# Opening of a gated linear-attention and GEGLU kernel: queries of two tiles by chunk, wq ahead of x tile 2, gate vector ahead of wk 1

## Chip, cores, metric

One Trainium2 chip, one core. The metric is the device time of one execution in microseconds; runs of a kernel are compared with runs of another from the same rounds on the same chip.

## The reference, cut to what matters

In outline (the attention is written as one call here):

```python
g = sigmoid((x * gate_w).sum(-1, keepdims=True))          # x: 2048 x 640, bf16
q, k, v = split(x @ wqkv)                                  # wqkv: 640 x 1920, 32 heads of 20
phi = lambda t: where(t > 0, t + 1, exp(t)) + 1e-6
a = linear_attention(phi(q), phi(k), v) @ wo
b = (gelu(x @ w_gate) * (x @ w_up)) @ w_down               # 640 x 1728, 1728 x 640
out = g * a + (1 - g) * b
```

Only the first 16 of 274 us matter here: the products of x with the key part (wk) and the query part (wq) of wqkv. The rows of wk and wq come in five chunks of 128 (wk 0 to 4, wq 0 to 4), because the 640-long contraction takes five matmuls. x is cut in 16 tiles of 128 rows, each wanted transposed. The gate vector becomes one more column of wq, which is why it is needed before the queries.

## The kernel before: the parts that the change touches

Each `P.op` puts an instruction into one engine's queue, in program order, and derives its semaphore waits. `eng="act"` puts a load into ScalarE's queue; the others go into SyncE's.

```python
NQ = 4                                     # tiles whose keys and queries are computed separately
...
# ScalarE: touch (a tiny first load), wk 1, wk 2, [table load], gate vector
# SyncE:   x 0, wk 0, x 1 (transposing load), wk 3, wk 4, x 2, x 3 (transposing), wq 0..4, x 4.. (transposing)
load_x(0); load_wk(0); load_xT(1); load_wk(3); load_wk(4)
load_wk(1, "act"); load_wk(2, "act")
P.op("act", lambda e: e.activation(eg[:, 0:1], zero, ACT.Exp), writes=[r_eg[0]])
P.op("dve", lambda e: e.memset(gw_sb, 0.0), writes=[r_gw])
dma_in(gw_sb[0:5, :], gate_w.rearrange("(k p) -> k p", p=128), [r_gw], eng="act")
for i in range(2, NQ): load_xT(i)
for k in range(KC):    load_wq(k)
for i in range(NQ, NT): load_xT(i)
...
warm(5, 512); warm(1, 128)                 # matmuls on constants, to bring TensorE's clock up
T(0, [0], 7); T(0, [1, 2, 3, 4], 6)        # x tile 0 is transposed by TensorE
warm(2, 128)
for k in range(3): KM(0, [k])              # keys of tile 0: a pair of matmuls (512 + 128 columns) per chunk
for k in range(3): KM(1, [k])              # keys of tile 1
KM(0, [3]); KM(1, [3]); gate_col(); KM(0, [4]); KM(1, [4])
for n in range(2 * NQ):
    if n in (2, 3): KM(n, ALLK)            # keys of tiles 2 and 3
    if n == NQ:
        for k in ALLK: QM(NQ, [k]); QM(NQ + 1, [k])   # queries of tiles 0 and 1, chunk by chunk
    if n > NQ + 1: QM(n, ALLK)             # queries of tiles 2 and 3
    phi1(n); phi2(n)                       # exp on ScalarE, the rest of phi on VectorE
for i in range(NQ, NT): KQ(i)              # fused tiles: keys and queries in 15 wide matmuls
```

## Time and profile before

| | before |
|---|---|
| time, median (range) of 6 runs | 274.00 us (273.52 to 275.16) |
| span of the profiled run | 272.6 us |
| TensorE busy | 267.6 us, 98% |
| first key pair / first fused tile starts | 4.45 us / 16.30 us |

The page of the kernel before: span, TensorE's busy time, and the engines of the chain of work that ended last.

```profile
span 272.6 us, 3416 instructions
PE 267.6 (98%) x1341; PEld 127.9 (47%) x1367; DVE 140.8 (52%) x247; ACT 75.9 (28%) x132; POOL 30.0 (11%) x28
PE 96%; DMA 1%; SPq 1%; issue 1%; DVE 0%
```

TensorE (PE) is the bound. A change can win only by removing stalls of PE. Here are its instructions in order of time, in the opening of the kernel before: start, duration, engine, line, operation, shapes, count, and in brackets the idle time before and what ended it. L453 is the wide matmul of a key pair, L539 a fused tile.

```profile
4.45 0.58 PE L453 MATMUL ps<-pool 128*128 128x512 bf16 x1 [0.48 <-DMA pool<-in_A_wqkv_dram]
...
4.93 0.51 PE L453 MATMUL ps<-pool 128*128 128x512 bf16 x1
...
5.34 0.38 PE L453 MATMUL ps<-pool 128*128 128x512 bf16 x1
...
5.61 0.38 PE L453 MATMUL ps<-pool 128*128 128x512 bf16 x1
...
7.27 0.38 PE L453 MATMUL ps<-pool 128*128 128x512 bf16 x1
...
8.12 0.39 PE L453 MATMUL ps<-pool 128*128 128x512 bf16 x1 [0.42 <-DMA pool<-in_A_x_dram]
...
16.30 1.03 PE L539 MATMUL ps<-pool 128*128 128x512 bf16 x4
```

Durations of matmuls overlap; the distance from start to start is the pace. A pair at full pace takes 0.27 us (5.34 to 5.61). Chunks 1 and 2 of wk were there when PE asked at 4.93 and 5.34 us (no wait shown). After the last key pair of tiles 0 and 1 (7.27 + 0.27 = 7.54) PE stood until 8.12 us for x tile 2: 0.58 us, the stall that the change aims at.

The queues that issue loads, SyncE's first, then ScalarE's, same kernel and columns:

```profile
1.71 1.30 SPq L353 DMA_TRANSPOSE pool<-in_A_x_dram  x1
3.06 1.04 SPq L341 DMA_DIRECT2D pool<-in_A_wqkv_dram  x2
4.14 2.53 SPq L353 DMA_TRANSPOSE pool<-in_A_x_dram  x2
6.72 2.48 SPq L341 DMA_DIRECT2D pool<-in_A_wqkv_dram  x5
```

```profile
1.24 0.93 ACTq L341 DMA_DIRECT2D pool<-in_A_wqkv_dram  x2
...
2.27 0.57 ACTq L341 DMA_DIRECT2D pool<-in_gate_w_dram  x1
```

And what the 16 DMA engines carried in the stretch from 3.6 to 4.2 us: queue, packets, MB, share of the 16 engines' time. q1 is SyncE's queue, q10 ScalarE's (wk 1 and 2, 256 packets in all).

```profile
DMA packets 215, 0.22 MB, mean 370 GB/s; under 512 B 46, under 2 KB 215, under 8 KB 215
...
q10 hardware_dynamic: 177, 0.20, 93.6%
q1 hardware_dynamic: 38, 0.02, 10.3%
```

### The profile page before, as it was taken

What the parts mean: (1) busy time and instruction counts of PE and PEld (TensorE: products, weight loads), DVE (VectorE), ACT (ScalarE), POOL (GpSimd) and SP (SyncE); (2) the same over time, 40 slices, a digit from 0 to 9 for tenths busy, and PEclk for the clock granted to TensorE, in tenths of its full rate; (3) what the DMA queues carried; (4) which work ended last, traced back from release to release, by engine and by line L of the source; (5) the groups of instructions that cost most, each with busy time, mean ns of one, the idle gap of its engine ahead of it and who ended that gap; (6) DMA issues with size and microseconds to landing.
All of it is one profiled execution on the core that took longest, in us unless ns stands there. A gap on an engine that the chain in (4) does not pass through costs nothing.

```text
span 272.6 us, 3416 instructions
## 1 busy us (share of the span) xinstructions
PE 267.6 (98%) x1341; PEld 127.9 (47%) x1367; DVE 140.8 (52%) x247; ACT 75.9 (28%) x132; POOL 30.0 (11%) x28
## 2 busy tenths in 40 slices
PE   8999999999999999999999999999999999999997
PEld 3555555544445454444444444444444444444444
DVE  1678989997233335999999999634210000000200
ACT  2455555210422453232222233224011122121021
POOL 5000000003240002242332422000000000000000
DMA  7976999600200011514121221273031110110211
GB/s 192 202 115 127 346 399 388 140 2 19 58 19 2 23 50 51 192 34 49 26 48 25 49 48 27 60 219 105 5 77 38 41 38 19 38 41 19 58 58 41
DMA packets 42864, 23.78 MB, mean 87 GB/s; under 512 B 32223, under 2 KB 41439, under 8 KB 42719
## 3 DMA queue, kind: packets, MB, share of 16 engines
q1 hardware_dynamic: 42517, 23.22, 31.9%
q10 hardware_dynamic: 330, 0.33, 0.3%
q8 instruction: 11, 0.18, 0.3%
q14 instruction: 6, 0.05, 0.1%
HBM read 13.83 MB, written 2.63 MB: 60 GB/s over the span
## 4 chain that ended last, share of the span: by engine, by line
PE 96%; DMA 1%; SPq 1%; issue 1%; DVE 0%
PE ps L700 41%; PE ps L864 23%; PE ps L539 12%; PE ps L596 6%; PE ps L843 4%; PE ps L468 2%; PE ps L811 2%; PE ps L678 2%; PE ps L599 1%; DMA pool<-in_A_x_dram 1%; PE ps L453 1%; PE ps L824 1%; SPq L341 1%; PE ps L721 1%; SPq L353 0%
## 5 line engine op out<-in xcount | busy, mean ns | idle before, releaser
L700 PE MATMUL ps<-pool 128*128 128x512 bf16 x510 | 113.0, 379 | 0.5
L700 PEld LDWEIGHTS ps<-pool 128*128 128x128 bf16 x520 | 50.5, 98 | 60.0
L864 PE MATMUL ps<-pool 128*128 128x512 bf16 (+2 forms) x300 | 62.4, 366 | 0.3
L706 ACT ACTIVATE pool<-ps 128x512 f32<-128x512 f32 x52 | 31.0, 597 | 73.1 <-PE ps L700 73.1
L708 DVE TENSOR_TENSOR pool<-ps,pool 128x512 bf16<-128x512 f32 x52 | 34.7, 689 | 31.7 <-PE ps L700 30.4
L864 PEld LDWEIGHTS ps<-pool 128*128 128x128 bf16 x306 | 29.2, 98 | 33.4 <-issue 0.4
L847 DVE TENSOR_TENSOR pool<-ps,pool 128x512 bf16<-128x512 f32 x4 | 2.8, 690 | 61.5 <-PE ps L843 61.5
L539 PE MATMUL ps<-pool 128*128 128x512 bf16 (+1 forms) x176 | 32.5, 343 | 0.2
L754 POOL TENSOR_TENSOR pool<-pool 128x640 f32<-128x640 bf16 x16 | 22.4, 1404 | 73.0 <-DVE pool L756 65.6
L871 ACT ACTIVATE pool<-ps,pool 128x512 bf16<-128x512 f32 (+1 forms) x16 | 10.9, 680 | 68.6 <-PE ps L864 68.6
L539 PEld LDWEIGHTS ps<-pool 128*128 128x128 bf16 x180 | 17.6, 98 | 15.0
L558 DVE SCALAR_TENSOR_TENSOR pool<-ps,pool 128x128 bf16<-128x128 f32 (+2 forms) x36 | 21.7, 602 | 2.1
L549 ACT ACTIVATE pool<-ps 128x640 bf16<-128x640 f32 x24 | 16.9, 703 | 15.8 <-DVE pool L558 9.3
L596 PE MATMUL ps<-pool 128*128 128x512 bf16 x76 | 19.2, 379 | 0.1
L764 DVE TENSOR_TENSOR pool<-pool 128x640 bf16<-128x640 bf16 x16 | 13.2, 826 | 0.6
L762 DVE TENSOR_SCALAR pool<-pool 128x32 f32<-128x32 f32 x16 | 12.8, 802 | 0.6
L756 DVE TENSOR_REDUCE pool<-pool 128x32 f32<-128x640 f32 x16 | 12.9, 808 | 0.0
L644 DVE TENSOR_TENSOR pool<-pool 128x640 f32<-128x640 f32 x14 | 11.6, 826 | 0.5
L843 PE MATMUL ps<-pool 128*128 128x512 bf16 x51 | 11.5, 379 | 0.1
L646 POOL PARTITION_ALL_REDUCE pool<-pool x1 | 4.0, 3971 | 61.0 <-DVE pool L644 61.0
L596 PEld LDWEIGHTS ps<-pool 128*128 128x128 bf16 x78 | 7.0, 98 | 7.3
L555 DVE TENSOR_SCALAR pool<-pool 128x640 bf16<-128x640 bf16 x24 | 7.9, 327 | 1.7 <-ACT pool L549 0.4
(70 smaller groups left out, 124.1 us busy)
## 6 DMA issues: line engine op xcount, KB each, us to landing
out_dram<-pool SPq DMA_DIRECT2D x19, 128.0 KB, 1.7
pool<-in_B_w_gate_dram SPq DMA_DIRECT2D x1, 2080.0 KB, 14.8
pool<-in_B_w_up_dram SPq DMA_DIRECT2D x1, 2080.0 KB, 18.0
pool<-in_A_wqkv_dram SPq DMA_DIRECT2D x8, 160.0 KB, 3.1
pool<-in_A_x_dram SPq DMA_DIRECT2D x1, 1280.0 KB, 9.2
pool<-in_A_x_dram SPq DMA_DIRECT2D x1, 1120.0 KB, 6.3
pool<-in_B_w_down_dram SPq DMA_DIRECT2D x1, 1120.0 KB, 6.4
pool<-omg_row SPq DMA_DIRECT2D x1, 1024.0 KB, 4.8
```

Of the source, the lines that this page charges most:

```text
L539: last = e.matmul(ps[:, b + p, 0:c1 - c0], xT[:, k, i * 128:(i + 1) * 128], wkq[:, k, c0:c1], start=(k == 0), stop=(k == KC - 1))
L549: P.op("act", lambda e: e.activation(e_buf[m], ps_flat[:, o:o + 640], ACT.Exp), reads=banks, writes=[r_e[m]])
L558: P.op("dve", lambda e, c0=c0, c1=c1: e.scalar_tensor_tensor(dst[:, c0:c1], ps_flat[:, o + c0:o + c1], 1.0 + EPS, e_buf[m][:, c0:c1], ALU. ...
L596: last = e.matmul(ps[:, b, :], pk[i][:, c * 128:(c + 1) * 128], x_aug[:, i, 0:512], start=(i == 0), stop=(i == NT - 1))
L700: last = e.matmul(ps[:, b, :], w[:, k, fc * 128:(fc + 1) * 128], xT[:, k, j * 512:(j + 1) * 512], start=(k == 0), stop=(k == KC - 1))
L706: P.op("act", lambda e: e.activation(ge[n], ps[:, gb, :], ACT.Gelu_apprx_tanh), reads=[bank[gb]], writes=[r_ge[n]])
L708: P.op("dve", lambda e: e.tensor_tensor(hT[fc][:, j * 512:(j + 1) * 512], ps[:, ub, :], ge[n], ALU.mult), reads=[bank[ub], r_ge[n]], write ...
L754: P.op("pool", lambda e: e.tensor_tensor(tmp[n], pq[i], z_b, ALU.mult), reads=[r_pq[i], r_zb], writes=[r_tmp[n]])
L756: P.op("dve", lambda e: e.tensor_reduce(den[n], tmp[n].rearrange("p (h d) -> p h d", h=32), AX.X, ALU.add), reads=[r_tmp[n]], writes=[r_de ...
L764: P.op("dve", lambda e: e.tensor_tensor(pq[i].rearrange("p (h d) -> p h d", h=32), pq[i].rearrange("p (h d) -> p h d", h=32), den[n].unsqu ...
L843: last = e.matmul(ps[:, b, :], wd[:, fc, 512:640], hT[fc][:, j * 512:(j + 1) * 512], start=False, stop=(fc == NFC - 2), skip_group_check=True)
L864: last = e.matmul(ps[:, pb, 0:c1 - c0], lhs, rhs, start=False, stop=(q == len(rows) - 1), skip_group_check=True)
```

## The change

The intent: PE has no use for x tile 2 before the queries of tiles 0 and 1, so fetch wq first, compute those queries right after the keys, and let x tiles 2 and 3 join the fused tiles. The gate vector is fetched earlier, because the queries now come earlier.

```diff
-NQ = 4
+NQ = 2
@@ loads
             P.op("act", lambda e: e.dma_start(touch[0:16, 0:4], A_wqkv[0:128:8, 640:644]),
                  writes=[P.res("touch")], dma=new_dma_key())
+            P.op("dve", lambda e: e.memset(gw_sb, 0.0), writes=[r_gw])
+            dma_in(gw_sb[0:5, :], gate_w.rearrange("(k p) -> k p", p=128), [r_gw], eng="act")
             load_x(0)
             load_wk(0)
             load_xT(1)
 ... (wk 3, wk 4; wk 1, wk 2 on ScalarE; the first activation)
-            P.op("dve", lambda e: e.memset(gw_sb, 0.0), writes=[r_gw])
-            dma_in(gw_sb[0:5, :], gate_w.rearrange("(k p) -> k p", p=128), [r_gw], eng="act")
-            for i in range(2, NQ):
-                load_xT(i)
             for k in range(KC):
                 load_wq(k)
-            for i in range(NQ, NT):
+            for i in range(2, NT):
                 load_xT(i)
@@ matmuls
             for n in range(2 * NQ):
-                if n in (2, 3):
-                    KM(n, ALLK)
                 if n == NQ:
                     for k in ALLK:
                         QM(NQ, [k])
                         QM(NQ + 1, [k])
-                if n > NQ + 1:
-                    QM(n, ALLK)
                 phi1(n)
                 phi2(n)
```

More of the change, by code (lines that the diff above doesn't have):

```diff
@@ L347, in load_x, with load_wk @@
                 dma_in(x_aug[:, i, 0:640], A_x[0, i * 128:(i + 1) * 128, :], [r_xn[i]], eng=eng)
-            def load_wk(k, eng="sp", after=()):
-                dma_in(wk[:, k, :], A_wqkv[k * 128:(k + 1) * 128, 640:1280], [r_wk[k]], reads=after, eng=eng)
+            def load_wk(k, eng="sp"):
+                dma_in(wk[:, k, :], A_wqkv[k * 128:(k + 1) * 128, 640:1280], [r_wk[k]], eng=eng)
             def load_xT(i, after=()):
@@ L355, in load_xT, with load_wq @@
                      reads=list(after), writes=[r_xT[i]], dma=new_dma_key())
-            def load_wq(k, eng="sp"):
-                dma_in(wq[:, k, 0:640], A_wqkv[k * 128:(k + 1) * 128, 0:640], [r_wq[k]], eng=eng)
+            def load_wq(k):
+                dma_in(wq[:, k, 0:640], A_wqkv[k * 128:(k + 1) * 128, 0:640], [r_wq[k]])
             P.op("act", lambda e: e.dma_start(touch[0:16, 0:4], A_wqkv[0:128:8, 640:644]),
                  writes=[P.res("touch")], dma=new_dma_key())
+            P.op("dve", lambda e: e.memset(gw_sb, 0.0), writes=[r_gw])
+            dma_in(gw_sb[0:5, :], gate_w.rearrange("(k p) -> k p", p=128), [r_gw], eng="act")
             load_x(0)
```

## The prediction

> **What bounds the kernel now.** The tensor engine: PE is busy 267.6 of 272.6 us (98%, the page), and the chain that ended last is 96% PE. Nearly all PE stalls lie in the first 8.1 us (timeline of PE): useful work starts at 4.45 us, when the first wk chunk lands (0.48 us waited); the keys of tiles 0 and 1 end at 7.54 us; then PE stands until 8.12 us for transposed x tile 2, about 0.58 us (the list of waits calls 0.42 of it). From 8.12 to 16.30 us, where the fused key-query tiles start, it streams six half tiles at 1.36 us; the stage table gives PE 8.33 of 8.40 us there and 32.29 of 32.50 in the fused tiles. So the ceiling of the change is about 0.6 us, 0.2%.
>
> **What the change does.** SyncE's queue (its timeline) issues wk 4 until 4.10 us, then x tiles 2 and 3 (4.14 to 6.67), then five wq chunks (6.72 to 9.20). Now wq goes first: issues of 0.5 us from 4.14 to 6.6 us, then x tile 2. Loads of wqkv take 3.1 us from issue to landing (median, DMA view), so wq 0 to 4 land at about 7.3 to 9.3 us; PE wants them at 7.6 to 9.8 (two query pairs of 0.27 per chunk). They fit by 0.3 to 0.5 us. These queries end near 10.4 us. x tile 2 lands 3.5 to 3.9 us after its issue begins, 10.1 to 10.5: a wait of 0 to 0.2 us. Later tiles come every 1.3 us, against 2.7 us of PE each. Later issues keep their times (tile 4 at 9.24 us).
>
> Tiles 2 and 3 move from separate halves (2 x 1.36 us) to the fused form (2.71 us per tile): equal for PE. VectorE pays 2.71 instead of 2.34 us per tile but keeps pace, and banks come free about 1 us before they are wanted.
>
> **The cost.** The gate vector's issue (0.57 us) goes ahead of wk 1 and 2 on ScalarE's queue, which were issued at 1.24 and 1.69 us and landed 3.2 us later, about 4.4 and 4.9, for use at 4.93 and 5.34. They now land at about 5.0 and 5.5. The DMA engines are full (share 1.08 in 4.4 to 8.1 us), so they interleave with x tile 1; the Trainium skill, "DMA: Bandwidth & Descriptors", section "Issuing engines are not separate DMA queues", says that all queues share the same 16 engines, and this trace agrees: around 3.4 to 4.2 us q10 moves while q1 nearly stops. wk 0 may land 0.1 to 0.2 us sooner. Net: the keys end 0.1 to 0.4 us later.
>
> **Sum.** 0.58 us removed, 0.25 given back at the keys, up to 0.1 at x tile 2: about 0.3 us gained, fused tile 4 starting at 15.9 to 16.2 us instead of 16.30. Later stages neither absorb nor amplify it. 274.05 - 0.3 = 273.7 us; before's own runs spread from 273.5 to 275.2. Range 272.7 to 274.9. Faster by over 2%: 0.01; same: 0.98; slower: 0.01.
>
> **What would show it.** The key matmul's wait for x gone, or a smaller one on the first fused tile near 10.4; new waits of 0.1 to 0.4 us for wk 1 or 2 near 5 us; none above 0.2 us on wq. PE busy unchanged at 267 to 268 us.
>
> **What would make it wrong.** wq landing later than 3.1 us after issue, so that the chunked queries trickle; x tile 2 landing after 11 us, behind wq; a clock dip in a longer stall; or wk 1 and 2 having more slack than I infer, which would give nearly the whole 0.6 us.

## The result

The changed kernel takes 276.98 us (median of 6 runs, 275.87 to 278.06) against 274.00. The ratio is 1.0107, 95% interval 1.0072 to 1.0142: about 3 us slower, outside the predicted range, with the sign of the forecast wrong. The profiled run is the slowest of the six (278.06), so its losses are larger than a typical run's; a second profile, shown with the experiments, fell on a typical one.

Page of the changed kernel, the same three lines:

```profile
span 276.8 us, 3427 instructions
PE 272.0 (98%) x1357; PEld 128.6 (46%) x1357; DVE 140.9 (51%) x249; ACT 75.9 (27%) x132; POOL 29.9 (11%) x28
PE 97%; DMA 2%; ACTq 0%; DVE 0%; issue 0%
```

PE is *busier* by 4.4 us although the program gives it ten fewer matmuls (tiles 2 and 3 take 15 each instead of 20; the page counts 1357 against 1341 because some matmul records are missing from a trace). PE's instructions in order of time, changed kernel (L451 key pair, L466 query pair, L533 fused tile):

```profile
3.79 0.61 PE L451 MATMUL ps<-pool 128*128 128x512 bf16 x1
...
5.28 0.58 PE L451 MATMUL ps<-pool 128*128 128x512 bf16 x1 [0.77 <-DMA pool<-in_A_wqkv_dram]
...
7.26 0.61 PE L451 MATMUL ps<-pool 128*128 128x512 bf16 x1 [1.29 <-DMA pool<-in_A_wqkv_dram]
...
7.77 0.63 PE L451 MATMUL ps<-pool 128*128 128x512 bf16 x1
...
8.30 0.64 PE L451 MATMUL ps<-pool 128*128 128x512 bf16 x1
...
11.53 0.63 PE L466 MATMUL ps<-pool 128*128 128x512 bf16 x1
...
13.13 0.41 PE L466 MATMUL ps<-pool 128*128 128x512 bf16 x1
...
13.43 0.38 PE L466 MATMUL ps<-pool 128*128 128x512 bf16 x1
...
15.07 9.15 PE L533 MATMUL ps<-pool 128*128 128x512 bf16 x49
```

Three things are to be seen. wk 0 comes earlier (first pair at 3.79 instead of 4.45), but wk 1 and 2 come at 5.28 and 7.26 us. After those waits a pair takes 0.53 us instead of 0.27 (7.77 to 8.30) until about 13.1 us. In this profile the pace did not fall, it had not risen yet: the very first wide matmul already takes 0.41 us from start to start (3.79 to 4.20), where a pair at full pace takes 0.27. And the wait for x tile 2 is indeed gone: fused tile 2 follows the last query at 15.07 without a gap.

The sum of the opening, before to after in these two profiles: first pair 0.66 us earlier; waits for wk 1 and 2 of 5.28 - 4.31 = 0.97 and 7.26 - 5.77 = 1.49 us; eleven pairs in 5.80 us (7.26 to 13.13, less 0.07 for the gate column) instead of 11 x 0.27 = 2.99, 2.8 us lost; the 0.58 us stall saved. That makes +4.0. The fused tiles confirm it: tile 4 starts two tiles of 2.71 us after 15.07, at 20.48, against 16.30, 4.2 us later, and the spans differ by 276.8 - 272.6 = 4.2 us. Nothing more happens afterwards.

The issuing queues of the changed kernel, SyncE's and ScalarE's:

```profile
1.71 1.30 SPq L353 DMA_TRANSPOSE pool<-in_A_x_dram  x1
3.06 3.41 SPq L341 DMA_DIRECT2D pool<-in_A_wqkv_dram  x7
6.51 19.34 SPq L353 DMA_TRANSPOSE pool<-in_A_x_dram  x14
```

```profile
1.24 0.57 ACTq L341 DMA_DIRECT2D pool<-in_gate_w_dram  x1
1.84 0.84 ACTq L341 DMA_DIRECT2D pool<-in_A_wqkv_dram  x2
```

These are as predicted: wk 1 and 2 are issued 0.6 us later. But the DMA engines in the same stretch, 3.6 to 4.2 us, look different:

```profile
DMA packets 245, 0.11 MB, mean 181 GB/s; under 512 B 198, under 2 KB 245, under 8 KB 245
...
q10 hardware_dynamic: 56, 0.06, 55.6%
q1 hardware_dynamic: 189, 0.05, 38.7%
```

Of wk 1 and 2, 56 packets moved instead of 177; 189 packets of SyncE's queue moved instead of 38, nearly all of them the small packets of the transposing load of x tile 1; and all engines together carried half as much.

The DMA view gives the time from issue to landing of each load. wk 1 took 3.3 us in both kernels (landed at 4.50 before, 5.14 after); wk 2 took 3.2 us before and 5.0 after (4.88 and 7.21). x tile 1, issued at 1.71 in both, took 3.8 and 5.4 us (5.53 and 7.11): with this traffic the keys of tile 1 could not have started before 7.1 us even with wk 2 on time. wk 0 landed 0.65 us earlier (4.31 and 3.66), and the transfer of x tile 1 behind it began earlier: packets under 512 B, 46 before and 198 after in the stretch shown. By 3.6 us wk 1 and 2 were not behind: ScalarE's queue moved 90 packets from 3.0 to 3.6 us, against 68 before. They fell behind after that, beside x tile 1.

### The profile page after: what moved, and what is told of

Same layout as the page of the kernel before. It is cut to its first block, busy times and chain, and to the rows that moved or that the text cites. A ratio compares the mean times of both kernels' runs of the same rounds, so it can differ in the third digit from the quotient of the medians.

```text
span 276.8 us, 3427 instructions
## 1 busy us (share of the span) xinstructions
PE 272.0 (98%) x1357; PEld 128.6 (46%) x1357; DVE 140.9 (51%) x249; ACT 75.9 (27%) x132; POOL 29.9 (11%) x28
## 4 chain that ended last, share of the span: by engine, by line
PE 97%; DMA 2%; ACTq 0%; DVE 0%; issue 0%
PE ps L694 41%; PE ps L858 23%; PE ps L533 14%; PE ps L590 6%; PE ps L837 4%; DMA pool<-in_A_wqkv_dram 2%; PE ps L672 2%; PE ps L805 2%; PE ps L593 1%; PE ps L451 1%; PE ps L466 1%; PE ps L818 1%; PE ps L715 1%; PE ps L733 0%; ACTq L341 0%; PE ps L452 0%
## 5 line engine op out<-in xcount | busy, mean ns | idle before, releaser
L694 PEld LDWEIGHTS ps<-pool 128*128 128x128 bf16 x520 | 50.4, 98 | 60.1
L858 PEld LDWEIGHTS ps<-pool 128*128 128x128 bf16 x306 | 29.1, 98 | 33.5 <-issue 0.4
L533 PE MATMUL ps<-pool 128*128 128x512 bf16 (+1 forms) x210 | 38.1, 344 | 0.0
L533 PEld LDWEIGHTS ps<-pool 128*128 128x128 bf16 x210 | 20.5, 98 | 17.5
L552 DVE SCALAR_TENSOR_TENSOR pool<-ps,pool 128x128 bf16<-128x128 f32 (+2 forms) x42 | 25.3, 602 | 2.8 <-DVE pool L549 0.5
L543 ACT ACTIVATE pool<-ps 128x640 bf16<-128x640 f32 x28 | 19.7, 703 | 17.9 <-DVE pool L552 11.1
L590 PEld LDWEIGHTS ps<-pool 128*128 128x128 bf16 x78 | 7.0, 98 | 7.2
L549 DVE TENSOR_SCALAR pool<-pool 128x640 bf16<-128x640 bf16 x28 | 9.1, 325 | 1.5
```

Source lines behind the costliest of these rows:

```text
L533: last = e.matmul(ps[:, b + p, 0:c1 - c0], xT[:, k, i * 128:(i + 1) * 128], wkq[:, k, c0:c1], start=(k == 0), stop=(k == KC - 1))
L543: P.op("act", lambda e: e.activation(e_buf[m], ps_flat[:, o:o + 640], ACT.Exp), reads=banks, writes=[r_e[m]])
L552: P.op("dve", lambda e, c0=c0, c1=c1: e.scalar_tensor_tensor(dst[:, c0:c1], ps_flat[:, o + c0:o + c1], 1.0 + EPS, e_buf[m][:, c0:c1], ALU. ...
L590: last = e.matmul(ps[:, b, :], pk[i][:, c * 128:(c + 1) * 128], x_aug[:, i, 0:512], start=(i == 0), stop=(i == NT - 1))
L694: last = e.matmul(ps[:, b, :], w[:, k, fc * 128:(fc + 1) * 128], xT[:, k, j * 512:(j + 1) * 512], start=(k == 0), stop=(k == KC - 1))
L858: last = e.matmul(ps[:, pb, 0:c1 - c0], lhs, rhs, start=False, stop=(q == len(rows) - 1), skip_group_check=True)
```

## The experiments

Theory I: the gate vector's issue, 0.57 us, pushed wk 1 and 2 out of the gap that they had to themselves and into the transfer of x tile 1; wk 2 lands 2 us later (wk 1 0.6), and PE then also runs at half rate for some us. Rivals: the five wq chunks queued by SyncE crowd them out (Q); the gate's own odd transfer does it, not its delay; the half rate comes from something else than idle time. All kernels gave correct results.

| run | runs, us | ratio to before (95%) |
|---|---|---|
| changed kernel, again | 274.41 to 277.47, median 276.79 | 1.0089 (1.0059 to 1.0119) |
| before, again (control) | 273.71 to 275.71, median 274.58 | 1.0020 (0.9998 to 1.0042) |
| changed, gate late | 274.00 to 274.44, median 274.13 | 1.0009 (0.9997 to 1.0021) |
| before, gate early | 274.66 to 277.76, median 276.55 | 1.0076 (1.0043 to 1.0109) |
| changed, second touch for the gate | 276.27 to 276.80, median 276.55 | 1.0094 (1.0081 to 1.0107) |
| changed, filler matmuls | 274.77 to 275.62, median 275.54 | 1.0052 (1.0040 to 1.0064) |
| changed, x 1 behind wk 4 | 275.08 to 278.94, median 276.92 | 1.0094 (1.0069 to 1.0119) |
| changed, x 1 plain | 274.07 to 276.74, median 275.35 | 1.0051 (1.0019 to 1.0083) |
| changed, SyncE holds | 277.48, one run | not timed |

### Gate vector late

```diff
 (changed kernel)
-            P.op("dve", lambda e: e.memset(gw_sb, 0.0), writes=[r_gw])     # ahead of wk 1
-            dma_in(gw_sb[0:5, :], gate_w..., [r_gw], eng="act")
 ... (wk 1, wk 2, first activation)
+            P.op("dve", lambda e: e.memset(gw_sb, 0.0), writes=[r_gw])
+            dma_in(gw_sb[0:5, :], gate_w..., [r_gw], eng="act")
```

> The changed kernel with only the gate vector's load put back behind wk 1 and 2 on ScalarE's queue. Theory I (the gate's 0.57 us issue pushed wk 1 and 2 into the transfer of x tile 1): wk 2 lands again near 4.9 us after the span's start instead of 7.2, the keys of tiles 0 and 1 end near 7.5 instead of 11.5, the opening gains its predicted 0.3 to 0.6 us, total 273.4 to 273.8 us, ratio to before 0.998 to 1.000. Rival Q (the five wq chunks queued by SyncE crowd out wk 2 on the shared engines): wk 2 still lands after 6.5 us, total 276 to 277.5 us, ratio 1.007 to 1.013.

Measured: 274.13 us, ratio 1.0009. The loss is gone, so Q falls: the same five wq chunks stand in SyncE's queue. The gain of 0.3 to 0.6 us did not come, which is the second question below. PE in this run:

```profile
5.78 0.39 PE L451 MATMUL ps<-pool 128*128 128x512 bf16 x1 [0.28 <-DMA pool<-in_A_x_dram]
...
6.98 0.39 PE L451 MATMUL ps<-pool 128*128 128x512 bf16 x1 [0.21 <-DMA pool<-in_A_wqkv_dram]
...
8.10 0.38 PE L466 MATMUL ps<-pool 128*128 128x512 bf16 x1
...
10.82 11.43 PE L533 MATMUL ps<-pool 128*128 128x512 bf16 x61
```

wk 1 and 2 cause no wait at all. New waits appear for x tile 1 at 5.78 and for wk 3 at 6.98; the queries start at 8.10, not 7.54.

### Gate vector early, nothing else

```diff
 (kernel before)
                  writes=[P.res("touch")], dma=new_dma_key())
+            (memset and load of the gate vector, moved here from behind the first activation)
```

> The kernel before with only the gate vector's load moved ahead of wk 1 and 2. Theory I: wk 2 lands near 7 us, tensor-engine waits of 1 to 2 us, then half-rate key matmuls; total 276 to 278 us, ratio to before 1.007 to 1.014. Rival Q: wk 1 and 2 come 0.6 us later at most, total 274.0 to 274.6, ratio 1.000 to 1.002.

Measured: median 276.55, ratio 1.0076; wk 2 at 6.94 us in the trace:

```profile
6.94 0.39 PE L453 MATMUL ps<-pool 128*128 128x512 bf16 x1 [1.33 <-DMA pool<-in_A_wqkv_dram]
```

Theory I again: this one load, moved alone, makes most of the loss. Two of the six runs were at 274.7 and four at 276.4 to 277.8.

### A second touch in the gate's place

```diff
 (changed kernel, gate vector late)
                  writes=[P.res("touch")], dma=new_dma_key())
+            P.op("act", lambda e: e.dma_start(touch[0:16, 4:8], A_wqkv[0:128:8, 644:648]),
+                 writes=[P.res("touch2")], dma=new_dma_key())
```

> The changed kernel with the gate vector behind wk 1 and 2 again, and a second copy of the tiny first load (16 rows of 8 bytes) in its place ahead of them: the same kind of delay of about 0.42 us in ScalarE's queue without the gate's five rows. If the delay alone does it (theory I): wk 2 lands after 6 us and the total is 275.5 to 277.5 us, ratio 1.005 to 1.013. If it is something of the gate's own transfer [...]: total 273.4 to 274.2 us, ratio 0.998 to 1.001.

Measured: 276.55 us, ratio 1.0094; wk 1 and 2 at 5.39 and 6.90 us. A delay of 0.5 us in ScalarE's queue by another tiny load does the same harm. So nothing peculiar to the gate's transfer is needed.

### Filler matmuls while wk 1 and 2 are under way

```diff
 (changed kernel)
-            for k in range(3):
-                KM(0, [k])
+            KM(0, [0])
+            warm(2, 512)
+            KM(0, [1])
+            warm(6, 512)
+            KM(0, [2])
```

> The changed kernel with filler matmuls (2 of 512 columns before the key matmuls of chunk 1, 6 before those of chunk 2, into a bank that is not in use yet), so that the tensor engine has no long idle time while wk 1 and 2 are under way. Theory C (most of the 3 us is the tensor engine running key and query pairs at 0.53 instead of 0.27 us after its idle time, as the profile of after shows from 7.26 to 13.1 us): pairs at 0.27 us from 7.3 us on, 2 to 3 us gained, total 273.8 to 275 us, ratio to before 1.000 to 1.004. Rival (the half rate is set by something else, for instance by the DMA traffic into the same memory): pairs stay at 0.53 us until about 13 us and the total at 276 to 278 us.

Measured: 275.54 us, ratio 1.0052. The fillers took 1.2 to 1.4 us off (against the two medians of the changed kernel, 276.79 and 276.98), less than the 2 to 3 expected: the first profile of the changed kernel was its slowest run, and the fillers ran on to 7.53 us although wk 2 had landed at 6.97. Pairs run at 0.27 us from 7.53 us on, with much the same DMA traffic as in the changed kernel (275 against 300 GB/s from 7.5 to 11 us), so the traffic does not set the rate. What the edit removed is the idle time before:

```profile
5.65 0.58 PE L451 MATMUL ps<-pool 128*128 128x512 bf16 x1 [0.20 <-DMA pool<-in_A_wqkv_dram]
...
7.53 0.38 PE L451 MATMUL ps<-pool 128*128 128x512 bf16 x1
...
7.80 0.38 PE L451 MATMUL ps<-pool 128*128 128x512 bf16 x1
```

### The changed kernel and the kernel before, again

No edit.

> The changed kernel, unchanged, beside the experiments: ratio 1.007 to 1.014, total 275.8 to 278 us, and a spread of about 2 us between its runs, because how long the half rate lasts after the idle time differs from run to run. wk 2 lands at 6.5 to 7.5 us in its profile.

> The kernel before, unchanged: a control for the noise of a ratio and a second profile of its opening. Ratio 0.998 to 1.002, total 273.7 to 274.3 us; keys of tiles 0 and 1 end at 7.4 to 7.7 us, the wait for x tile 2 is 0.3 to 0.8 us. If the opening differs by more than that between two profiles of one kernel, differences of 0.3 us between kernels can't be read from one profile.

Measured: changed 276.79 (ratio 1.0089), a spread of 3 us; wk 1 and 2 at 5.20 and 6.91 us. In this profile PE had reached full rate (5.20), and the clock records show the fall. Stage table: stretch, length, busy times (instructions) of PE, PEld, DVE, ACT, POOL, then granted clock, DMA share, GB/s.

```profile
core 0: us, PE busy (x) PEld busy (x) DVE busy (x) ACT busy (x) POOL busy (x), PEclk, DMA share, GB/s
7.70:11.00 3.30, 3.30 (x16) 1.65 (x15) 0.32 (x2) 0.87 (x2) 0.00 (x0) 0.50 1.09 267
11.00:13.50 2.50, 2.50 (x20) 1.39 (x18) 2.07 (x4) 0.49 (x2) 0.00 (x0) 0.97 0.77 129
```

The clock falls well after PE had resumed at 6.91; asked with finer stretches, the table gives 0.50 from 7.73 to 11.14, for 3.41 us, and then full. The Trainium skill, "TensorE: Matmul & The Clock Gate", section "Part 1: The HAM clock gate (the "warmup" mystery)", describes this: the clock halves after an idle window of about 3.4 us, is restored after a busy one, and the window is free-running, so it differs from run to run. The length agrees: the half-rate stretch lasts 3.41 us here, in the profile of "gate early" (7.82 to 11.23) and in that of "SyncE holds" (8.29 to 11.70). The spread of the runs fits too. But PE was not idle for such a window: in the 3.41 us before the fall (4.32 to 7.73) it was busy for 1.48 us, and no gap was longer than 1.44. This profile's fused tiles start at 13.50 instead of 15.07; its span is 275.3, 2.7 us over before.

The control: ratio 1.0020, but runs up to 275.71, and its profile (that slowest run) shows pairs at 0.53 us from 4.72 to about 9.5 us after a wait of 0.70 us for wk 0. So the kernel before draws the same lot, less often: 5 of its 57 runs lie above 274.9 us. The expectation for its opening (keys done by 7.7 us) was missed by 2 us, and 0.3 us can't be read from one profile each.

### x tile 1 behind wk 4; x tile 1 without a transposing load

Theory X: what slows wk 1 and 2 is the transposing load of x tile 1 beside them. Rival R: any backlog on SyncE's queue does.

```diff
 (changed kernel, first of the two)
             load_wk(0)
-            load_xT(1)
             load_wk(3)
             load_wk(4)
+            load_xT(1)
 (changed kernel, second of the two)
-NXN = 1
+NXN = 2
-            load_xT(1)
+            load_x(1)
 ... (tile 1 transposed by TensorE after KM(0, [0]), into banks 5 and 4)
+            T(1, [0], 5)
+            T(1, [1, 2, 3, 4], 4)
```

> The changed kernel with the transposing load of x tile 1 issued behind wk 3 and 4 instead of ahead of them; the gate vector stays ahead of wk 1 and 2. Theory X (wk 1 and 2 are slow because they share the DMA engines with the transposing load, whose small packets halve what the engines move): wk 2 lands at 5.2 to 5.8 us; keys of tile 1 then wait for x tile 1 near 6 us; keys end by 8.5; total 274 to 275 us, ratio 1.000 to 1.004. Rival R (any backlog on SyncE's queue slows them, whatever its packets): wk 2 lands after 6.5 us, total 276 to 278 us.

> The changed kernel with x tile 1 loaded plainly, as tile 0 is, and transposed by the tensor engine (5 more small matmuls and two copies on VectorE, about 0.4 us of PE); the same bytes on the same queue, but no transposing load before x tile 2. Theory X: wk 2 lands at 5.2 to 5.7 us with the gate still ahead of it, nothing waits over 0.6 us, total 273.6 to 274.6 us, ratio 0.998 to 1.002. Rival R (it is the backlog of bytes): wk 2 lands after 6.5 us, total 276 to 278 us.

Measured: with x tile 1 behind wk 4, wk 1 came at 6.31 and wk 2 at 7.15 us; with x tile 1 plain, wk 2 came at 6.14. The first result is what rival R said and rules out theory X as stated; the second (275.35 us, wk 2 at 6.14) lies between the two. In both, wk 1 and 2 met plain packets of SyncE's queue first and moved at about half the engines' rate; with x tile 1 plain the two queues moved 197 packets each from 3.6 to 5.0 us, at 330 GB/s together:

```profile
DMA packets 394, 0.46 MB, mean 330 GB/s; under 512 B 33, under 2 KB 394, under 8 KB 394
...
q1 hardware_dynamic: 197, 0.23, 50.5%
q10 hardware_dynamic: 197, 0.23, 47.7%
```

The transposing load makes the total smaller (188 GB/s in the same stretch of the changed kernel), but beside plain loads too wk 1 and 2 got only half. The spread of the times (275.08 to 278.94 and 274.07 to 276.74) is probably the clock's; that was not checked run by run.

### SyncE holds until wk 1 and 2 have landed

```diff
 (changed kernel)
             load_wk(0)
-            load_xT(1)
+            load_wk(1, "act")
+            load_wk(2, "act")
+            load_xT(1, after=r_wk[1:3])        # SyncE waits for both here
```

> The changed kernel, gate vector ahead of wk 1 and 2, but SyncE's queue stops before x tile 1 until wk 1 and 2 have landed, so that nothing but the two of them moves. Not meant to be fast. If wk 1 and 2 are late because SyncE's loads share the DMA engines with them: wk 2, issued at 2.3 us, now lands 2.6 to 3.3 us after its issue, at 4.9 to 5.6 us, against 6.9 to 7.3 us in two profiles of the changed kernel. If they are late for a reason of their own (issued behind the gate on ScalarE's queue): wk 2 lands after 6.5 us still. x tile 1 then comes near 8.5 to 9 us and the total is 276 to 279 us.

Measured, one run:

```profile
4.69 0.45 PE L451 MATMUL ps<-pool 128*128 128x512 bf16 x1
...
5.03 0.38 PE L451 MATMUL ps<-pool 128*128 128x512 bf16 x1
...
8.03 0.40 PE L451 MATMUL ps<-pool 128*128 128x512 bf16 x1 [2.57 <-DMA pool<-in_A_x_dram]
```

The pair of wk 2 starts at 5.03 us, 2 us earlier than in the changed kernel, with the gate vector still ahead of it; SyncE's held load is issued at 5.00. By the DMA view wk 2 was issued at 2.23 and landed at 4.92, 2.7 us later. So issuing wk 2 at 2.2 us instead of 1.7 costs nothing by itself. Sharing the DMA engines costs the 2 us. The hold takes all of SyncE's later loads away at once, so it does not say which of them costs how much. The Trainium skill, "DMA: Bandwidth & Descriptors", section "Queues, rings and completion order", says that each DMA engine takes turns between the queues that have work, a packet at a time; the even splits beside plain loads agree (197 to 197 with x tile 1 plain, 158 to 158 in the same stretch with x tile 1 behind wk 4). Beside the transposing load the counts were uneven, 56 to 189, so there such turns are not what the profile's packet counts show. (The rest of this kernel is slow, as meant.)

### Where the expected gain went

With the gate put back, the new order of SyncE's queue should still have saved the 0.58 us stall. Four runs of two kernels looked for it; "filler" is one more matmul of 512 columns before the first key pair, meant to have the clock up in both.

```diff
             warm(2, 128)
+            warm(1, 512)
```

> The kernel before with that one filler matmul. Its second profile showed pairs at 0.53 us until 9.5 us (span 274.4), its first at 0.27 from 5.3 us on (span 272.6), so the same draw of the clock is in it. Filler theory: always 0.27 from about 5.3 us on, spread of the runs under 0.6 us, mean 273.7 to 274.0 us, ratio 0.998 to 1.000. Rival: spread and mean as before, 273.6 to 275.7, ratio 1.000 to 1.002.

> The changed kernel with the gate vector behind wk 1 and 2, and that one filler matmul; beside the kernel before with the filler, it shows what the new order of SyncE's queue alone is worth with the clock up in both. If the wait for x tile 2 (0.58 us) is really saved: 0.3 to 0.6 us below that run. Rival (the keys' own loads now land later, x tile 1 at 5.7 and wk 3 at 6.9 us, and give it back): within 0.2 us of it.

> The kernel before with the one filler matmul, again: a second sample for a small difference. If the filler is worth something: runs within 0.5 us of each other, ratio 0.998 to 1.000 again, no pair at 0.53 us after 5.7 us. If the first run was luck: runs up to 275.5 us appear as in the control. x tile 1 lands by 5.7 us.

> The changed kernel with the gate late and the filler, again: a second sample for what the queue order is worth. Give-back theory: x tile 1 lands again at 5.6 us or later, and wk or wq chunks make further waits of 0.2 us or more; typical run 0.1 to 0.4 us above the run of before with the filler. If the first profile was luck: x tile 1 by 5.6 us, the fused tiles start by 10.5 us, and the typical run is 0.2 us or more below that run.

| run | runs, us | ratio to before (95%) |
|---|---|---|
| before + filler | 273.61 to 273.80, median 273.73 | 0.9992 (0.9979 to 1.0005) |
| before + filler, again | 273.77 to 274.25, median 273.97 | 1.0003 (0.9991 to 1.0015) |
| changed, gate late + filler | 273.96 to 277.35, median 274.14 | 1.0027 (0.9994 to 1.0060) |
| changed, gate late + filler, again | 273.72 to 275.56, median 274.20 | 1.0021 (1.0003 to 1.0038) |

The gain is not there: the kernel with the new order is 0.4 and 0.2 us *above* the old order by the medians of the same rounds. (Of the slowest run, 277.35 us, more than 1 us lies outside the profiled span, which was 274.5 us long; in most runs the two differ by 1.3.) Its second profile shows small waits in place of the one:

```profile
5.66 0.39 PE L451 MATMUL ps<-pool 128*128 128x512 bf16 x1 [0.20 <-DMA pool<-in_A_x_dram]
...
8.44 0.39 PE L466 MATMUL ps<-pool 128*128 128x512 bf16 x1
...
10.82 8.29 PE L534 MATMUL ps<-pool 128*128 128x512 bf16 x45
```

x tile 1 is waited for until 5.66, wq 1 until 8.44 (the query pair before it started at 8.01 and takes 0.27), and the fused tiles begin at 10.82, so fused tile 4 at 10.82 + 2 x 2.71 = 16.24; in the second profile of before with the filler it starts at 16.10. Without the work on tiles 2 and 3 as a buffer, PE asks for each load of the opening as it lands, and the saving comes back as several waits of 0.1 to 0.4 us in this profile, up to 0.6 in the first (x tile 1 at 6.33, wq 1 at 9.20 us). There was also less to save than 0.58 us: with the filler the kernel before stood only 0.37 us (7.60 to 7.97) and 0.10 us (7.82 to 7.92) for x tile 2 in its two profiles, because the tile landed earlier (7.92 and 7.87 instead of 8.07) and, in the second, PE came later (7.82 instead of 7.54). And in the old order a wait for x tile 1 or wk 3 only shortens the stall for x tile 2 behind it, while in the new one the waits add up. No experiment separates these parts. That the wq traffic behind them makes x tile 1 and wk 3 land later is suggested and not shown: x tile 1 landed at 5.53 to 5.83 us in four profiles of the old order and at 5.61, 5.73 and 6.28 in three of the new one with the gate late, wk 3 at 6.28 to 6.47 and at 6.33, 6.92 and 6.93.

The filler in the kernel before gave no slow draw in ten runs, where the kernel before had 5 in 57 (275.16, 275.86, and three of the control's six above 274.9). None in ten is no proof at that rate, and the mean is not clearly below that of before.

Two more kernels tried to beat both: gate late and x tile 1 plain, without and with the filler.

```diff
 (both: gate vector late, NXN = 2, load_x(1), T(1, ...) as above; the second also warm(1, 512))
```

> The changed kernel with the gate vector back behind wk 1 and 2 and x tile 1 loaded plainly and transposed by the tensor engine. If the late landing of x tile 1 (5.7 us in the run with the gate late) held the keys back, they now end at 7.6 to 7.9 us instead of 8.1, the fused tiles start at 10.3 to 10.6 instead of 10.82, total 273.4 to 273.9 us, ratio 0.998 to 1.000. If wk 1 and 2 merely share the engines with other plain loads instead (as with the gate ahead and x tile 1 plain, where wk 2 came at 6.1 us): keys end at 8.0 to 8.4 us, ratio 1.000 to 1.004.

> The same with one more filler matmul of 512 columns before the first key matmul, to keep the tensor engine busy while wk 0 lands. If the half rate is set by idle time: no pair at 0.53 us after 5.5 us, spread of the runs under 0.6 us, total 273.3 to 273.9 us. If not: the spread stays over 1 us.

Measured: 274.03 us (ratio 1.0029, 1.0000 to 1.0059) and 274.39 (1.0024, 1.0002 to 1.0046), with runs up to 276.3. PE waited for x tile 1 until 5.42 and 6.27 us. The filler did not keep the spread under 0.6 us. In its profile the idle time had moved behind it (1.27 us before 6.27), but no pair after that took 0.53 us, so why some runs are slow is not shown. No version beat the kernel before.

## Why the prediction was wrong, point by point

- **What bounds the kernel, and the ceiling of 0.6 us**: right. Nothing outside the first 16 us changed, and the shift at the fused tiles (4.2 us) equals the shift of the span.
- **SyncE's order and issue times**: right (seven chunks from 3.06 to 6.47, x tile 2 at 6.51). The wait for x tile 2 vanished, as said. Fused tiles cost PE the same.
- **The step that failed** is in "The cost": "They now land at about 5.0 and 5.5", "Net: the keys end 0.1 to 0.4 us later". PE got them at 5.28 and 7.26 us (5.20 and 6.91 in the second profile), and the keys ended 4 us later (about 2.9 in the second). I took the 3.2 us from issue to landing as a constant and moved it by 0.57 us. For wk 1 it held (3.3 us, landed at 5.14); wk 2 took 5.0 us, and x tile 1, which the prediction left where it was, 5.4 instead of 3.8. The constant holds for both chunks only while SyncE's queue is nearly idle from 3.6 to 4.2 us, as the packet counts of before show (177 against 38). In the changed kernel wk 0 landed 0.65 us sooner (the prediction had 0.1 to 0.2), x tile 1 started sooner, and wk 1 and 2 shared the engines with it and with what followed. The hold experiment shows that sharing, not the issue delay, is the cost: wk 2 for PE at 5.0 against 6.9 to 7.3 us. I quoted the very sentence about shared engines and put a small part of its price on it.
- **The half rate** was listed under what would make the prediction wrong ("a clock dip in a longer stall") and not priced. It made 2.8 us in the profiled run and about 1.6 us in a typical one: in the second profile six pairs took 0.53 instead of 0.27 us. With fillers that part went away.
- **The sum**: "0.58 us removed ... about 0.3 us gained" would not have come even without the gate. With the gate late the kernel is at 1.0009 of before. The saved stall returned as small waits on x tile 1, wk 3 and wq. The wq chunks did not "fit by 0.3 to 0.5 us": wq 1, put at about 7.8 us, came at 8.44 and 9.20 us in the two profiles where PE was early enough to ask for it. It is the same mistake: in these profiles wq 1 took 3.8 and 4.5 us from issue to landing, not 3.1.
- What stays open: why, within the shared stretch, the last packets of wk 2 trail so far behind (a few packets per 0.2 us until 6.6 us), and how much of the later landing of x tile 1 is the queue order and how much chance.

## What to carry to other kernels

A load's time from issue to landing belongs to the schedule it was measured in: before moving a load by half a microsecond, look at which queue has the DMA engines in the window it leaves and in the window it enters. When the first loads of a kernel feed the tensor engine directly, price a stall with the half-rate pace that may follow it, not only with its length. A stall at the end of a stretch may be the slack that hides the loads before it; taking the work out that followed it can expose each of them.

## What the Trainium skill lacked or had wrong

- "TensorE: Matmul & The Clock Gate", section "Why this matters for your kernels", asks for no idle gaps over about 3 us. Here two gaps of 0.81 and 1.44 us (4.39 to 5.20 and 5.47 to 6.91) within about 2.5 us were followed by 3.41 us at clock 0.50. In the control pairs stayed at 0.53 us for 4.8 us after a wait of 0.70 us, where the first profile of the same kernel, with a wait of 0.48 us, was at full pace from about 5.3 us. So gaps well under 3 us were not safe in this opening; whether their length or their place in the window decides is not shown.
- The same page, section "Seeing it yourself", warns that clock records are not to be trusted one by one. Here they were missing rather than wrong: the profile of the changed kernel has none (its page has no PEclk line), and the stage table then gives 1.00 for 7.26 to 13.10 us, where pairs ran at 0.53 us. Where there are records, as in the table above, they fit the pace. The pace from start to start is the safer reading.
- "DMA: Bandwidth & Descriptors", section "Issuing engines are not separate DMA queues", says that issuing from several engines saves only issue time. It has no number for what a plain load loses beside other loads: here 56 instead of 177 packets in 0.6 us beside a transposing load, with 181 instead of 370 GB/s for all engines together, and wk 2 landing 2.3 us later.
- The same page's section "Anatomy of one DMA — SWDGE (gpsimd) path" has a fit for loads issued by GpSimd, 2.0 us plus bytes over bandwidth, which as an estimate gives 2.4 us for 160 KB; there is none for loads issued by ScalarE or SyncE, and none for loads that share the engines. Here one 160 KB load from ScalarE's queue, wk 2, took 2.7 us with SyncE's queue held (issued at 2.23, landed at 4.92), 3.2 us in a nearly free window (1.71 to 4.88), and 5.0 us beside other loads (2.23 to 7.21).
